# Attention and two feed-forward stages on one core: scores a slot earlier, banks emptied before the splits, three operands read in parts

## The chip, the core and the metric

The kernel runs on one core of one Trainium2 chip. TensorE (PE in the rows; PEld is its weight load) multiplies matrices into PSUM banks, VectorE (DVE), ScalarE (ACT) and GpSimd (POOL) work on tiles in SBUF, and SyncE (SP, SPq for its queue) issues the transfers. The metric is the device time of one execution in microseconds, lower is better; of several runs the median is given.

## The reference, cut to what matters

```
# attention: 4 batches x 8 heads, 768 rows of 64; chunks of 32 rows see 16 rows to the left, 8 to the right, 8 memory rows
for c in range(S // 32):
    k_full = concat([mem_k, k[:, :, max(0, 32*c - 16) : min(S, 32*c + 40)]])     # v_full alike
    a = softmax(scale * q[:, :, 32*c : 32*c + 32] @ k_full.T)
    out[:, :, 32*c : 32*c + 32] = a @ v_full
x = out, heads side by side                      # 3072 x 512
h = x @ w_in                                     # 512 -> 2048, weights in float64
x1 = softplus(h) @ w_out                         # max(h, 0) + log1p(exp(-|h|)); 2048 -> 512
a, b = x1 @ w_a, x1 @ w_b                        # 512 -> 1536 each
result = (a * b) @ w_out2                        # 1536 -> 512, float32
```

## The kernel before, in words

Every fp32 product is made of three products of rounded halves: a value is kept as a high part and a low part, and high x high, high x low and low x high are added in PSUM. So each operand has to be split: ACT writes the high part (a copy that rounds), DVE or POOL the low part (a subtraction). Weights arrive as float64 and are converted on chip: a rounding step on ACT (`top`), two bit operations on DVE (`value`), then the split (`high` on ACT, `low` on DVE).

The 3072 tokens go through in stages, with their times in the profiled execution:

- Head, 0 to 56 us: the six 64-token blocks of the first 384 tokens (class `Block`, order in the table `ROUND`), as a pipeline of scores, softmax, transposes (`flip`, tile `pat`), values (`pxb`) and `place`. `Block.place` (L380) writes the high part of x (L384) and a plain copy `xrb` (L386) on ACT and the low part on DVE (L387); `Block.store` sends `xrb` to the scratch array `x_scratch` in DRAM (L390). `FILL` adds idle-filling matmuls.
- First pass, tiles 0 to 7 of 384 tokens, 56 to 504.6 us (the last end of it 482 to 504.6): for the hidden blocks f = 0 to 9, `emit_h` (tile `ph`), `emit_soft` (softplus: three ACT steps into `e`, L591 to L593, then DVE's `g`, L595, then the split into `gh` and `gl`, L572 and L575) and `emit_x1` (tiles `px`, L608, two blocks behind). Beside that the attention of the tile that comes next runs as three 128-token units (class `Unit`) whose steps have slots, two per f, in `STEPS`, `SECOND` and `EARLY_STEPS`: `turn`, `scores` (two banks, `sc`), `soft` (eight reads of these banks by DVE, L399, and eight exponentials by ACT, L403), `norm`, `flip` (into `af`), `values` (tile `pxa`, L500), `place` (L502) and `store`. The banks of `sc`, `pa` and `pxa` share one tag, `att`, with two buffers. At the end of a tile four DVE copies (L616) take `px` out into two buffers of `e` and two of `g`, and four DMAs send them to `x_part_scratch`.
- Middle, pairs 0 to 2 of 512 + 512 tokens, 504.6 to 782.2 us: the hidden blocks 10 to 15, two at a time, by seven products in place of eight (`h_step`, three per pair; tiles `hX`, `hY`, `hW`, `hV`, L799), softplus on four results that go through two halves of one tile `et` (L894 to L899) and are split by `soft_split` (L901), and their products with `w_out` (`x1_products`, tiles `pz`, L970), to which the stored part is added (`part`, L973). The seven operands of the next pair are made from loaded x (`load_pair`, `add_pair`, `split_hi`, `split_lo`, L681).
- Pair phase, pairs 3 to 5, 782.2 to 1332.3 us: twelve `pair_step` per pair for the second feed-forward stage; on the first of them (782.2 to 964 us) the twelve weight blocks are also combined and split.

Conversion of w_a, w_b and w_out2 into `v_scratch` (class `Early`, L693: a fetch, `top` L707 on ACT, `value` L711 and L712 on DVE, a store) is spread over the first pass and the middle; `weigh` there converts w_out's blocks 10 to 15.

What sets the order: SP, PE and DVE run in the order in which the code writes their work (a `manual_schedule`), ACT and POOL too in tile 0 and from tile 7 on; between them the compiler places ACT and POOL. In the middle `order()` hangs steps on points `at(0)` to `at(12)` of an `h_step` by `put((p, s, k), ...)`. All DMAs named here go out from SP in one row, and each waits for the one eight before it (the semaphores `DMAHW0` to `DMAHW7`).

## Time and profile before

| what | value |
|---|---|
| runs shown | 1337.58, 1342.11, 1336.69 us; median 1337.58 |
| profiled execution | 1334.09 us, its span 1332.30 us |
| PE busy | 1189.3 us, 89% |
| DVE busy | 828.4 us, 62% |
| ACT busy | 559.5 us, 42% |
| POOL busy | 384.8 us, 29% |
| DMA | 226.40 MB, mean 170 GB/s |

How to read it: PE is busy through most of the span, so what can be gained lies in the stretches where it stands or runs at a lower granted clock. The view by windows gives for each stretch the busy time of each engine, the granted TensorE clock as a share of full speed and the DMA share; the view of waits gives the idle time ahead of an instruction and what released it; the timeline gives single instructions.

### The profile page before, as it was taken

Reading aid. Unit: us, or ns where it says so; the run is one execution under the profiler, and the core shown is the slowest. Engines: PE = TensorE matmul, PEld = TensorE weight load, DVE = VectorE, ACT = ScalarE, POOL = GpSimd, SP = SyncE. Lnnn points to the kernel's source line nnn. Section 1 sums busy time; section 2 is a strip of 40 time slices with the busy share of each in tenths; the row PEclk is TensorE's granted clock in tenths of the full one; section 3 lists DMA queues with packets and bytes.
Section 4 is the critical chain, followed back from the end, with each engine's and each line's share of the span. In section 5 each row is a group of like instructions: output and inputs, shape, how many; then the busy total and the mean of one; then the engine's idle time right before and its main releaser. Section 6 shows DMA issues by size and latency. Waiting matters only on the chain.

```text
span 1332.3 us, 19883 instructions
## 1 busy us (share of the span) xinstructions
PE 1189.3 (89%) x7120; PEld 1020.3 (77%) x7120; DVE 828.4 (62%) x1641; ACT 559.5 (42%) x1314; POOL 384.8 (29%) x300
## 2 busy tenths in 40 slices
PE   8588889899899987759769589999999999999999
PEld 5488879788898986547557468888888888888887
DVE  5574666566676486675575675668754666646555
ACT  5585656565675555453536524222311112221110
POOL 1000234332333473261344666547100111000000
PEclk9798999999999999779979889999999999999999
DMA  9574555464533442555756758575386643475411
GB/s 250 142 175 78 124 129 118 109 142 105 134 86 110 158 170 107 189 217 170 260 171 231 247 203 308 190 285 195 137 274 232 211 136 127 152 283 175 148 56 64
DMA packets 222643, 226.40 MB, mean 170 GB/s; under 512 B 125984, under 2 KB 165328, under 8 KB 222544
## 3 DMA queue, kind: packets, MB, share of 16 engines
q1 hardware_dynamic: 222160, 225.08, 53.3%
q8 instruction: 56, 0.92, 0.3%
q14 instruction: 43, 0.35, 0.1%
q0 software_dynamic: 384, 0.05, 0.0%
HBM read 155.09 MB, written 69.99 MB: 169 GB/s over the span
## 4 chain that ended last, share of the span: by engine, by line
PE 58%; issue 13%; ACT 8%; DMA 7%; DVE 6%; POOL 5%; SPq 3%; POOLq 0%; DVEq 0%; ACTq 0%
PE py L822 15%; PE pW L799 7%; PE pX L799 7%; PE pV L799 7%; PE ph L584 7%; PE px L608 6%; PE pY L799 4%; ACT sm L403 3%; POOL g L904 2%; PE pz L970 2%; DMA x<-x_scratch 1%; DVE af L471 1%; PE pxa L500 1%; DMA raw_b<-in_moe_w_b_dram 1%; DMA raw_a<-in_moe_w_in_dram 1%
## 5 line engine op out<-in xcount | busy, mean ns | idle before, releaser
L822 PE MATMUL py<-w2o,c 128*128 128x512 f32 (+1 forms) x870 | 218.0, 388 | 0.0
L584 PE MATMUL ph<-x,w 128*128 128x384 f32 x960 | 188.3, 345 | 11.4 <-ACT x L514 10.3
L822 PEld LDWEIGHTS py<-w2o,c 128*128 128x128 f32 x870 | 162.6, 188 | 33.5
L584 PEld LDWEIGHTS ph<-x,w 128*128 128x128 f32 x960 | 171.0, 193 | 16.2 <-ACT x L514 11.5
L608 PE MATMUL px<-gh,w 128*128 128x384 f32 x640 | 180.2, 342 | 3.0 <-DVE xo L616 1.5
L970 PE MATMUL pz<-g,w 128*128 128x512 f32 x432 | 117.2, 432 | 50.7 <-DVE part L973 29.7
L875 ACT CAST c<-r 128x512 fp32r<-128x512 f32 x36 | 22.4, 621 | 303.4 <-DVE r L873 303.4
L970 PEld LDWEIGHTS pz<-g,w 128*128 128x128 f32 x432 | 90.5, 212 | 75.9 <-DVE part L973 30.9
L608 PEld LDWEIGHTS px<-gh,w 128*128 128x128 f32 x640 | 117.9, 189 | 7.3 <-issue 3.8
L595 DVE SCALAR_TENSOR_TENSOR g<-ph,e 128x384 f32<-128x384 f32 x80 | 44.5, 556 | 116.9 <-ACT e L593 116.1
L608 PE MATMUL px<-gl,w 128*128 128x384 f32 x320 | 108.1, 338 | 5.3 <-DVE gl L575 5.1
L831 DVE TENSOR_TENSOR y<-py,y 128x512 f32<-128x512 f32 (+1 forms) x121 | 82.9, 685 | 35.8 <-PE py L822 35.6
L575 POOL TENSOR_TENSOR gl<-g,gh 128x384 fp32r<-128x384 f32 x60 | 60.9, 1015 | 148.1 <-ACT gh L572 122.8
L904 POOL TENSOR_TENSOR g<-et,g 128x512 fp32r<-128x512 f32 x36 | 48.1, 1346 | 143.8 <-ACT g L903 143.8
L471 DVE STREAM_TRANSPOSE af<-sm 32x256 f32<-32x256 f32 x180 | 78.1, 434 | 2.6
L572 ACT CAST gh<-g 128x384 fp32r<-128x384 f32 x80 | 41.1, 513 | 66.9 <-DVE g L595 66.3
L591 ACT ACTIVATE e<-ph 128x384 f32<-128x384 f32 x80 | 38.9, 486 | 70.8 <-PE ph L584 42.0
L872 DVE TENSOR_TENSOR d<-pW,q 128x512 f32<-128x512 f32 x36 | 24.9, 691 | 68.6 <-PE pW L799 68.6
L608 PEld LDWEIGHTS px<-gl,w 128*128 128x128 f32 x320 | 60.7, 190 | 6.6 <-DVE gl L575 6.1
L403 ACT ACTIVATE sm<-sm,st 128x96 f32<-128x96 f32 x168 | 60.4, 363 | 3.4 <-DVE st L399 3.4
L758 POOL TENSOR_TENSOR u<-t,u 128x512 fp32r<-128x512 f32 x30 | 43.2, 1445 | 43.6 <-ACT u L754 43.6
L799 PE MATMUL pW<-xs,u 128*128 128x512 f32 x216 | 54.8, 389 | 0.0
(203 smaller groups left out, 2347.1 us busy)
## 6 DMA issues: line engine op xcount, KB each, us to landing
...
```

Of the source, the lines that this page charges most:

```text
L403: nc.scalar.activation(sm[:, h], sm[:, h], AF.Exp, bias=st[:, 0, h:h + 1], scale=-1.0, accum_out=st[:, 1, h:h + 1])
L471: nc.vector.transpose(out=af[32 * kb:32 * kb + 32, x], in_=self.sm[32 * x:32 * x + 32, :, 32 * kb:32 * kb + 32])
L575: engine.tensor_tensor(lo, val, hi.bitcast(F32), ALU.subtract)
L584: nc.tensor.matmul(ph, lhsT=w[:, a, kt * P:(kt + 1) * P], rhs=x[:, c, kt, :], start=n == 0, stop=n == 3 * KT - 1)
L595: nc.vector.scalar_tensor_tensor(g, ph, 0.0, e, ALU.max, ALU.add)
L608: nc.tensor.matmul(acc[t][i][:, :TT], lhsT=a, rhs=c, start=f == 0 and m == 0, stop=f == FA - 1 and m == 2)
L758: engine.tensor_tensor(u[:, :, 1], self.source(i), u[:, :, 0].bitcast(F32), ALU.subtract)
L799: nc.tensor.matmul(bank[:, :T2], lhsT=u[:, j, a, kt * P:kt * P + P], rhs=x[kt][:, c], start=first_ and m == 0, stop=m == 3 * KH - 1, skip_ ...
L822: nc.tensor.matmul(b, lhsT=c[:, x, r], rhs=w[:, y, cols], start=n == 0, stop=n == 3 * GROUP - 1)
L831: tt(y, b, y, ALU.add)
L904: nc.gpsimd.tensor_tensor(g[:, 1], e, g[:, 0].bitcast(F32), ALU.subtract)
L970: nc.tensor.matmul(b[:, :T2], lhsT=a, rhs=c, start=f == FA and m == 0, stop=f == NF1 - 1 and m == 2)
```

## The change

The change has six parts.

1. Tables. The scores of the units come a slot or more earlier, the third unit is placed at slot 17 of a tile (18 before), and the steps of the first six units have new slots. The conversion halves that ran inside the first units' softmax (`weigh` of class `Unit`) are gone from there; `convert()` runs them all.
2. `Unit.place` writes the low part from PSUM on DVE for every tile; before, it did so for t < 2 only, and POOL did it from the plain copy for the others.
3. `Block.place` makes no plain copy on ACT. POOL adds the two parts into spare buffers, and `store_first` sends them to `x_scratch` in three DMAs at slot 1 of tile 0. One half of `packed[1]` loads into the buffers of `loaded[0]`.
4. `store_parts` sends the two parts of x of each tile to a new scratch array (two DMAs of 786 KB per tile), and `load_parts` reads the operands "11", "12" and "22" of pairs 0 to 2 from it as parts. For these no `split_hi` and `split_lo` remain; of the other four, ACT writes all the high parts and DVE all the low ones.
5. `h_step` has two `et` tiles (four halves); the softplus steps that read PSUM stand ahead of the splits, and the low parts go to POOL and DVE in turn.
6. In the middle, `load_pair` and `add_pair` of the next pair come earlier, one `Early` conversion is made per `h_step` in place of two to four, and the remaining 15 move to the first eight steps of the pair phase. `weigh` runs three times in tile 7 (two before) and three times in pair 0 (four before).

```
-PLACED = (5, 12, 18)
+PLACED = (5, 12, 17)
-STEPS = {0: ((-13, "turn"), (-9, "scores"), (-8.9, "soft"), (-7, "norm"), (-5, "flip"), ...
+STEPS = {0: ((-13, "turn"), (-10, "scores"), (-9.9, "soft"), (-8, "norm"), (-6, "flip"), ...
...
     class Block:
             nc.scalar.copy(xh, self.px)
-            self.raw = raw = wp.tile([P, KT, QB], F32, tag="w", name=f"xrb{u}")
-            nc.scalar.copy(raw, self.px)
             nc.vector.tensor_tensor(xl, self.px, xh.bitcast(F32), ALU.subtract)
-        def store(self):
-            nc.sync.dma_start(xd[:, :, QB * self.u:QB * self.u + QB], self.raw)
+            n, k, i = [x[u] for x in ((3, 3, 3, 2, 2, 1), (0, 0, 0, 1, 1, 2), (0, 1, 2, 0, 1, 0))]
+            if i == 0:
+                pool, tag = ((a2, "kt"), (a2, "qt"), (wp, "w"))[k]
+                first[k] = pool.tile([P, KT, n * QB], F32, tag=tag, name=f"xrb{u}", **({"bufs": 1} if k < 2 else {}))
+            nc.gpsimd.tensor_tensor(first[k][:, :, i * QB:i * QB + QB], xh.bitcast(F32), xl.bitcast(F32), ALU.add)
...
     class Unit:
-            if t < 2:
-                nc.scalar.copy(xh, self.px)
-                nc.vector.tensor_tensor(xl, self.px, xh.bitcast(F32), ALU.subtract)
-                nc.scalar.copy(raw, self.px)
-            else:
-                nc.scalar.copy(raw, self.px)
-                nc.scalar.copy(xh, self.px)
-                nc.gpsimd.tensor_tensor(xl, raw, xh.bitcast(F32), ALU.subtract)
+            nc.scalar.copy(xh, self.px)
+            nc.vector.tensor_tensor(xl, self.px, xh.bitcast(F32), ALU.subtract)
+            nc.scalar.copy(raw, self.px)
...
+    def store_first():
+        for k, c0, n in ((0, 0, 3 * QB), (1, 3 * QB, 2 * QB), (2, 5 * QB, QB)):
+            nc.sync.dma_start(xd[:, :, c0:c0 + n], first[k])
+    def store_parts(t):
+        for c in range(2):
+            nc.sync.dma_start(xhl[:, :, c, TT * t:TT * t + TT], xt[t][:, c].bitcast(F32))
+    plan.append((1, -1, store_first))
+    plan += [(2 * FA * t + 1.1, -1, partial(store_parts, t)) for t in range(NTILE - 1)]
...
+    def load_parts(p, n):
+        sums[p, n] = operand(p, n)
+        t, k = {"11": (0, 0), "12": (0, 1), "22": (1, 1)}[n]
+        c0 = (2 * p + t) * T2
+        (x,) = sums[p, n]
+        for i in range(KH):
+            nc.sync.dma_start(x[:, i].bitcast(F32), xhl[:, KH * k + i, :, c0:c0 + T2])
...
     def h_step(p, s, at, between):
-        et = wp.tile([P, 2, T2], F32, tag="w", name=f"et{p}_{s}")
+        es = [wp.tile([P, 2, T2], F32, tag="w", name=f"et{p}_{s}_{n}") for n in range(2)]
         product(x, p, f, "12", False)
         soft_e(x, e1)
         soft_g(r, e0)
-        soft_split(p, 1, f1, e0)
         at(4)
         product(w, p, f, "22", False)
         tt(d21, w, q, ALU.add)
+        soft_hi(p, 1, f1, e0)
+        soft_lo(p, 1, f1, e0, nc.gpsimd)
+        soft_e(d21, e2)
+        soft_g(x, e1)
         at(5)
         product(v, p, f, "s4", False)
         tt(q, v, q, ALU.add)
-        soft_g(x, e1)
-        soft_e(d21, e0)
-        soft_split(p, 0, f0, e1)
-        soft_g(d21, e0)
-        soft_e(q, e1)
-        soft_split(p, 1, f0, e0)
-        soft_g(q, e1)
-        soft_split(p, 0, f1, e1)
+        soft_hi(p, 0, f0, e1)
+        soft_e(q, e3)
+        soft_lo(p, 0, f0, e1, nc.vector)
+        soft_g(d21, e2)
+        soft_hi(p, 1, f0, e2)
+        soft_lo(p, 1, f0, e2, nc.gpsimd)
+        soft_g(q, e3)
+        soft_hi(p, 0, f1, e3)
+        soft_lo(p, 0, f1, e3, nc.vector)
...
         for p in range(NPAIR):
-                for k in (0, 2) + (() if s + 1 < NS else (5, 7)):
-                    if pre:
-                        e = pre.pop(0)
-                        put((p, s, k), e.fetch)
-                        put((p, s, k + 4), e.top, e.value)
-                        put((p, s, k + 5), e.store)
-            put((p, NS - 1, 1), partial(load_pair, p + 1))
-            for k, n in ((7, "11"), (8, "s2"), (8, "s3"), (9, "s1"), (10, "12"), (11, "22"), (12, "s4")):
+                e = pre.pop(0)
+                put((p, c, 1), e.fetch)
+                put((p, c, 6), e.top, e.value)
+                put((p, c, 8), e.store)
+            put((p, 1, 5), partial(load_pair, p + 1))
+            if p + 1 < NPAIR:
+                for k, n in ((1, "11"), (5, "12"), (6, "22")):
+                    put((p, 2, k), partial(load_parts, p + 1, n))
+                names = ((7, "s2"), (8, "s3"), (11, "s1"), (12, "s4"))
...
+        for n, e in enumerate(pre):
+            for k, step in ((0, e.fetch), (3, e.top), (4, e.value), (5, e.store)):
+                k += 7 * (n // 2) + 2 * (n % 2)
+                put(("g", k // 7, k % 7), step)
```

Three places in the order, before and after. The rows give the line, the operation with its tiles and shapes, and the semaphores waited for.

First the end of the head. On SP before (`raw` is a weight in float64, `kn` keys of a later tile, the `xrb` rows left out are the other four of six):

```order
L116 DMA raw_196<-in_moe_w_out_dram 128x1024 [waits DMAHW4_49]
L390 DMA x_scratch<-xrb_432 512x1x64 [waits DMAHW5_49,Activation_49]
...
L390 DMA x_scratch<-xrb_638 512x1x64 [waits DMAHW2_49,Activation_49]
L116 DMA raw_655<-in_moe_w_in_dram 128x4x256 [waits DMAHW3_49,DVE_49]
L116 DMA raw_738<-in_moe_w_out_dram 128x1024 [waits DMAHW4_49,PE_49]
L201 DMA kn_78<-in_k_dram 32x12x32 [waits DMAHW5_49]
```

On SP now:

```order
L117 DMA raw_194<-in_moe_w_out_dram 128x1024 [waits DMAHW4_49]
L117 DMA raw_644<-in_moe_w_in_dram 128x4x256 [waits DMAHW5_49,PE_49,Activation_49]
L549 DMA x_scratch<-xrb_431 512x1x192 [waits DMAHW6_49,Pool_49]
L549 DMA x_scratch<-xrb_587 512x1x128 [waits DMAHW7_49,Pool_49]
L549 DMA x_scratch<-xrb_629 512x1x64 [waits DMAHW0_49,Pool_49]
L117 DMA raw_730<-in_moe_w_out_dram 128x1024 [waits DMAHW1_49,DVE_49,PE_49]
L553 DMA x_parts_scratch<-x_428 512x1x384 [waits DMAHW2_49,Activation_49]
L553 DMA x_parts_scratch<-x_428 512x1x384 [waits DMAHW3_49,DVE_49]
```

And DVE there, before (`work` holds a block's scores and sums, `scb` is the bank of its scores; the last block):

```order
L407 TENSOR_SCALAR work_375<-work_375 128x4 [waits Activation_49]
L408 RECIPROCAL work_375<-work_375 128x4 [waits DVE_49]
L410 TENSOR_TENSOR work_375<-work_375 128x384 [waits DVE_49]
L387 TENSOR_TENSOR x_430<-pxb_479,x_430 128x4x64 [waits PE_49,Activation_49]
L399 ISA work_438<-scb_439,mask_72 128x96 [waits DMAHW5_49]
```

DVE at the same place now:

```order
L412 TENSOR_SCALAR work_373<-work_373 128x4 [waits Activation_49]
L413 RECIPROCAL work_373<-work_373 128x4 [waits DVE_49]
L415 TENSOR_TENSOR work_373<-work_373 128x384 [waits DVE_49]
L390 TENSOR_TENSOR x_428<-pxb_477,x_428 128x4x64 [waits Activation_49]
L404 ISA work_436<-scb_437,mask_72 128x96
```

A block's `work` took the buffer of an `xrb` that a DMA was still reading, and DVE waited for that DMA; now no wait for a DMA stands there.

Second the end of a tile of the first pass, on DVE before (`xo` and `g` from `px` are the tile's results on their way out, `ph_2` the third hidden block of the next tile, `sc_10` a bank of scores):

```order
L595 SCALAR_TENSOR_TENSOR g<-ph_1_2221,e_1_2234 128x384 [waits Activation_49,Pool_49]
L471 STREAM_TRANSPOSE af<-sm_2093 32x256 [waits PE_49]
L471 STREAM_TRANSPOSE af<-sm_2093 32x256 x4
L616 COPY xo_0_2258<-px_0_1648 128x384 [waits DMAHW3_49,DVE_49,PE_49]
L616 COPY xo_1_2261<-px_1_1649 128x384 [waits DMAHW4_49,DVE_49,PE_49]
L616 COPY g<-px_2_1650 128x384 [waits PE_49,Pool_49]
L616 COPY g<-px_3_1651 128x384 [waits PE_49,Pool_49]
L595 SCALAR_TENSOR_TENSOR g<-ph_2_2286,e_2_2299 128x384 [waits DMAHW4_49,DVE_49,Activation_49]
L399 ISA sm_2306,st_2307<-sc_10_2268,mask_72 128x96 [waits DMAHW5_49,PE_49]
```

DVE at the same place now:

```order
L476 STREAM_TRANSPOSE af<-sm_2077 32x256 x5
L601 SCALAR_TENSOR_TENSOR g<-ph_1_2222,e_1_2235 128x384 [waits Activation_49,Pool_49]
L622 COPY xo_0_2274<-px_0_1667 128x384 [waits DMAHW4_49,DVE_49,PE_49]
L622 COPY xo_1_2277<-px_1_1668 128x384 [waits DMAHW5_49,DVE_49,PE_49]
L622 COPY g<-px_2_1669 128x384 [waits PE_49,Pool_49]
L622 COPY g<-px_3_1670 128x384 [waits PE_49,Pool_49]
L404 ISA sm_2284,st_2285<-sc_10_2244,mask_72 128x96
```

The reads of `sc_10` stood behind the `g` of `ph_2`; now they stand ahead of it.

Third the end of pair 0, on DVE before (`val` is a converted weight, `x`, `xs`, `xa` are operands of pair 1, `part` the sums over the hidden blocks):

```order
L899 SCALAR_TENSOR_TENSOR et_2_5994<-hq_2_6002,et_2_5994 128x512 [waits DVE_49,Activation_49]
L711 TENSOR_SCALAR val_o_6106<-raw_o_6031 128x512 [waits DMAHW3_49]
L712 SCALAR_TENSOR_TENSOR val_o_6106<-raw_o_6031,val_o_6106 128x512 [waits DVE_49,Activation_49]
L681 TENSOR_TENSOR x_1_6129<-x_1_6014,x_1_6129 128x2x512 [waits DMAHW7_49,Activation_49]
L711 TENSOR_SCALAR val_a_6165<-raw_a_6076 128x512 [waits DMAHW7_49,DMAHW6_49]
L712 SCALAR_TENSOR_TENSOR val_a_6165<-raw_a_6076,val_a_6165 128x512 [waits DVE_49,Activation_49]
L681 TENSOR_TENSOR xs_1_6148<-x_1_6018,xs_1_6148 128x2x512 [waits Pool_49]
L973 TENSOR_TENSOR part_0_0_6044<-pz_0_0_5962,part_0_0_6044 128x512 [waits DMAHW4_49,PE_49]
```

DVE at the same place now:

```order
L913 SCALAR_TENSOR_TENSOR et_2_1_5999<-hq_2_6007,et_2_1_5999 128x512 [waits DVE_49,Activation_49]
L921 TENSOR_TENSOR g_0_15_6099<-et_2_1_5999,g_0_15_6099 128x512 [waits Activation_49]
L725 TENSOR_SCALAR val_o_6103<-raw_o_6019 128x512 [waits DMAHW1_49]
L726 SCALAR_TENSOR_TENSOR val_o_6103<-raw_o_6019,val_o_6103 128x512 [waits DVE_49,Activation_49]
L695 TENSOR_TENSOR xs_1_6123<-xs_6021,xs_1_6123 128x2x512 [waits Activation_49]
L695 TENSOR_TENSOR xs_1_6141<-x_1_5937,xs_1_6141 128x2x512 [waits Activation_49]
L994 TENSOR_TENSOR part_0_0_6049<-pz_0_0_5969,part_0_0_6049 128x512 [waits DMAHW4_49,DMAHW3_49,PE_49]
```

Between the last softplus and the first `part` stood two conversions and two low parts of operands; now stand there a low part of the softplus, one conversion and two low parts of operands.

## Rows read from the trace of the kernel before

**Rows 1.** Windows, one a stage: length, busy (x instructions) by engine, PEclk, DMA share, GB/s.

```profile
0.00:56.00 56.00, 34.16 (x449) 25.54 (x449) 25.95 (x129) 25.76 (x83) 5.95 (x19) 0.82 0.76 202
56.00:125.00 69.00, 59.20 (x624) 55.86 (x624) 47.09 (x130) 51.69 (x134) 2.16 (x4) 0.93 0.59 135
125.00:482.00 357.00, 326.23 (x2739) 308.47 (x2737) 218.69 (x696) 219.24 (x650) 127.70 (x111) 0.99 0.48 122
482.00:504.60 22.60, 17.46 (x97) 16.50 (x97) 22.50 (x22) 9.06 (x20) 15.87 (x11) 1.00 0.66 241
504.60:605.10 100.50, 69.72 (x261) 54.60 (x260) 66.93 (x76) 51.06 (x85) 39.52 (x22) 0.81 0.45 158
605.10:693.70 88.60, 67.62 (x271) 53.08 (x270) 54.77 (x58) 41.70 (x68) 32.22 (x18) 0.90 0.58 205
693.70:782.20 88.50, 67.96 (x272) 53.34 (x271) 54.63 (x58) 45.63 (x76) 48.06 (x31) 0.88 0.62 220
782.20:964.00 181.80, 181.80 (x804) 150.54 (x803) 124.60 (x164) 58.17 (x106) 97.44 (x78) 1.00 0.62 229
```

**Rows 2.** Waits of the head, all engines: total us, times, longest us.

```profile
PE pat L370 <- ACT x L384: 20.2, 2, 19.7
...
DVE work L399 <- DMA x_scratch<-xrb: 18.0, 1, 18.0
```

**Rows 3.** Timeline of the head: start, us, instruction, idle time before and releaser.

```profile
36.38 12.80 SPq L390 DMA_DIRECT2D x_scratch<-xrb  x3
44.90 0.26 DVE L399 CUSTOM_DVE_ANT_0 work<-scb,mask 128x96 f32<-128x96 f32 x1 [17.98 <-DMA x_scratch<-xrb]
...
48.47 1.06 PE L370 MATMUL pat<-ident,work 128*96 128x128 f32 x4 [19.66 <-ACT x L384]
```

**Rows 4.** Waits of PE in tiles 0 to 7.

```profile
PE pxa L500 <- issue: 21.9, 8, 4.8
PE ph L584 <- ACT x L514: 10.3, 4, 3.5
```

**Rows 5.** Timeline at the start of tile 3.

```profile
197.24 0.49 ACT L591 ACTIVATE e<-ph 128x384 f32<-128x384 f32 x1 [4.35 <-DMA x_part_scratch<-xo]
...
198.87 0.56 DVE L595 SCALAR_TENSOR_TENSOR g<-ph,e 128x384 f32<-128x384 f32 x1 [2.28 <-ACT e L593]
199.34 0.25 DVE L399 CUSTOM_DVE_ANT_0 sm<-sc,mask 128x96 f32<-128x96 f32 x1
...
200.23 0.98 PE L500 MATMUL pxa<-af,vn 96*64 96x64 f32 x26 [2.57 <-issue]
```

**Rows 6.** Waits of PE in the middle.

```profile
PE pz L970 <- DVE part L973: 29.7, 3, 10.3
PE hX L799 <- ACT hq L915: 14.4, 4, 10.2
PE pz L970 <- POOL g L904: 12.9, 3, 5.6
```

**Rows 7.** Timeline of DVE at the end of pair 0.

```profile
579.31 1.52 DVE L711 TENSOR_SCALAR val_o<-raw_o 128x512 uint32<-128x512 uint32 x1
...
582.45 3.41 DVE L681 TENSOR_TENSOR x<-x,x 128x1024 fp32r<-128x1024 f32 x1
585.78 2.58 DVE L711 TENSOR_SCALAR val_a<-raw_a 128x512 uint32<-128x512 uint32 x1
588.47 2.67 DVE L712 SCALAR_TENSOR_TENSOR val_a<-raw_a,val_a 128x512 uint32<-128x512 uint32 x1
...
594.33 2.47 DVE L973 TENSOR_TENSOR part<-pz,part 128x512 f32<-128x512 f32 x4
...
601.80 0.42 DVE L711 TENSOR_SCALAR val_b<-raw_b 128x512 uint32<-128x512 uint32 x1
602.32 0.69 DVE L712 SCALAR_TENSOR_TENSOR val_b<-raw_b,val_b 128x512 uint32<-128x512 uint32 x1
...
605.88 1.22 DVE L681 TENSOR_TENSOR xb<-x,xb 128x1024 fp32r<-128x1024 f32 x1
```

More of the change, by code (lines that the diff above doesn't have):

```diff
@@ L29 @@
              (0, "place"), (1, "store")),
-         2: ((-13, "turn"), (-9, "scores"), (-8.9, "soft"), (-7, "norm"), (-5, "flip"), (-3, "flip2"), (-0.1, "values"),
-             (0, "place"), (0.9, "store"))}
-SECOND = (((15, "turn"), (20, "scores"), (20.1, "soft"), (22, "norm"), (23, "flip"), (25, "flip2"), (26.9, "values"),
+         2: ((-12, "turn"), (-8, "scores"), (-7.9, "soft"), (-6, "norm"), (-4, "flip"), (-3, "flip2"), (-0.1, "values"),
+             (0, "place"), (1, "store"))}
+SECOND = (((15, "turn"), (19, "scores"), (19.1, "soft"), (21, "norm"), (22, "flip"), (24, "flip2"), (26.9, "values"),
@@ L41 @@
+EARLY_STEPS = (((4, "scores"), (4.1, "soft"), (5, "normal"), (8, "flip_p"), (10.9, "values"), (11, "place"), (12, "store")),
+               ((6, "scores"), (6.1, "soft"), (7, "normal"), (12, "flip_p"), (13.9, "values"), (14, "place"), (15, "store")),
+               ((9, "scores"), (9.1, "soft"), (10, "normal"), (15, "flip_p"), (16.9, "values"), (17, "place"), (18, "store")))
 EARLY = len(EARLY_STEPS)
-FETCHED = (2, 3, 4, 5)
+FETCHED = (3, 4, 5, 6)
 ROUND = ((2, "normal"), (4, "place"), (None, "top"), (0, "scores"), (1, "soft"), (None, "low"), (None, "value"),
-         (2, "flip"), (3, "values"), (None, "high"), (4, "store"))
+         (2, "flip"), (3, "values"), (None, "high"))
@@ L276, in load @@
             t = self.t
-            kp = wp.tile([P, 4, 4, D], F32, tag="w", name=f"kp{t}_{half}")
-            qp = wp.tile([P, 4, 4, D], F32, tag="w", name=f"qp{t}_{half}")
+            if t == 1 and half == 0:
+                kp, qp = [x.rearrange("p k n s -> p (k n s)")[:, :1024].rearrange("p (h r d) -> p h r d", h=4, r=4)
+                          for x in (loaded[0].k, loaded[0].q)]
+            else:
+                kp = wp.tile([P, 4, 4, D], F32, tag="w", name=f"kp{t}_{half}")
+                qp = wp.tile([P, 4, 4, D], F32, tag="w", name=f"qp{t}_{half}")
             self.raw[half] = kp, qp
@@ L909, in h_step @@
         f0, f1 = FA + 2 * s, FA + 2 * s + 1
-        et = wp.tile([P, 2, T2], F32, tag="w", name=f"et{p}_{s}")
-        e0, e1 = et[:, 0], et[:, 1]
+        es = [wp.tile([P, 2, T2], F32, tag="w", name=f"et{p}_{s}_{n}") for n in range(2)]
+        e0, e1, e2, e3 = [es[n // 2][:, n % 2] for n in range(4)]
         x = bank("acc3" if (p, s) == (0, 1) else "h", f"hX{p}_{s}")
@@ L1065, in order @@
         LAST = NTILE - 1
-        for s, at in ((0, 3), (1, 6)):
-            put(("t", at - 3), cvs[NF2 + s].fetch)
-            for k, step in enumerate(cvs[NF2 + s].slots()):
+        for c, at in ((0, 3), (1, 6)):
+            put(("t", at - 3), cvs[NF2 + c].fetch)
+            for k, step in enumerate(cvs[NF2 + c].slots()):
                 put(("t", at + k), step)
-        for n, at in ((0, 2), (1, 4)):
+        for n, at in ((0, 2), (1, 4), (2, 8)):
             put(("t", at), partial(weigh, FA + n, ("t", at + 4), ("t", at + 5), ("t", at + 7), ("t", at + 8)))
-        put(("t", 1), partial(load_pair, 0))
+        put(("t", 1), partial(store_parts, LAST), partial(load_parts, 0, "11"), partial(load_pair, 0))
@@ L1078, in order @@
+        put(("t", 10), partial(load_parts, 0, "12"))
         put(("t", 17), cvs[NF2 + 2].fetch)
[L1080 to L1082 removed]
+        put((0, 0, 0), partial(load_parts, 0, "22"))
+        put((0, 0, 2), partial(split_hi, 0, "s4", nc.scalar.copy), partial(split_lo, 0, "s4", nc.vector))
         for k, step in enumerate(cvs[NF2 + 2].slots()):
@@ L1107, in order @@
+            for k, n in names:
+                put((p, 2, k), partial(split_hi, p + 1, n, nc.scalar.copy))
+                low = partial(split_lo, p + 1, n, nc.vector)
+                if n != "s4":
+                    put((p, 2, k), low)
                 elif p + 1 < NPAIR:
                     put((p + 1, 0, 0), low)
-            put((p, NS - 1, 3), partial(load_part, p, 0))
-            put((p, NS - 1, 9), partial(load_part, p, 1))
-        assert not pre
+            put((p, 2, 3), partial(load_part, p, 0))
@@ L1112, in order @@
+            put((p, 2, 9), partial(load_part, p, 1))
         P2 = NPAIR - 1
@@ L1179, in at @@
                     if p == NPAIR:
+                        run("g", f, k)
                         for g, kk in ((f + 1, 7 + k), (f + 2, k)):
@@ L1216, in order @@
                         x1_products(NPAIR - 1, 1, i, range(FA, NF1))
+        assert not todo, sorted(todo)
         while jobs:
```

58 lines of the change are left out of this document (25 added, 33 removed).

## The prediction, made before the changed kernel ran

> **What bounds the kernel now.** I read the windows first, one for each stage [rows 1]. PE is busy in 1189.3 of 1332.3 us, so the question is where the other 143 are, and where PE runs at a lower granted clock. The first pass of the pair phase (782.2 to 964) has neither: 181.80 of 181.80 us busy at clock 1.00, 804 matmuls, that is 0.226 us each. This is my measure for a full matmul. The head leaves PE idle for 56.0 − 34.2 = 21.8 us, tile 0 for 9.8, tiles 1 to 7 for 30.8, the end of the first pass for 5.1, pairs 0, 1 and 2 for 30.8, 21.0 and 20.5. In the pairs the granted clock is 0.81 to 0.90 besides: 261 matmuls at 0.226 are 59.0 us where pair 0 takes 100.5, so 41.5 are lost; pairs 1 and 2 lose 27.4 and 27.0 in the same way. Of these 95.9 us, 72.3 are idle and 23.6 are matmuls at a lower clock (an estimate, as some matmuls are narrower and some records may be missing).
>
> Then I read the waits and the timeline at the places where PE stands. In the head one wait carries nearly all: PE stands 19.7 us because a block's softmax is late, and that because DVE waited 18.0 us for a store of `xrb` [rows 2]. The timeline shows why [rows 3]: three of the six stores are issued from 36.38 on, behind the weight fetches in SP's row, and DVE reads the scores of the last block only at 44.90. In the first pass PE waits 21.9 us ahead of `pxa`, eight times, and 10.3 us for the x of the next tile [rows 4]. One such place is shown [rows 5]: ACT's `e` waits 4.35 us for the store of `xo`, DVE's `g` behind it starts at 198.87, the reads of the score bank behind that at 199.34, and PE, which needs the bank, at 200.23, 2.57 us late. In the middle three waits make 57.0 of the 72.3 idle us: `part` on DVE 29.7, `hq` on ACT 14.4, the low parts on POOL 12.9 [rows 6].
>
> **The change part by part.** The sum is made against the profiled execution, 1334.1 us (its span of 1332.3 and 1.8 around it); the median of the runs stands 3.5 above it.
>
> Head: −18. No buffer that DVE needs is read by a store any more, so the 18.0 us of DVE's wait [rows 2] go. POOL gets six additions and works 5.95 of 56 us there [rows 1], ACT loses six copies. The three stores wait for POOL, in SP's row behind weight fetches; behind them stand more weights and the parts of x, which nothing needs within the next tile. What is late next is the fetch of the first weights; it isn't bounded by a row better than by the wait itself, so the term lies between 0 and −19.7.
>
> Tile 0: −8. Idle 9.8 us plus 7% of 69 us at clock 0.93, some 4.8 [rows 1]. The conversions leave the first units' softmax, yet they all still have to be made by ACT, which is busy 51.7 of 69 us. I take about half; bounds 0 and −13.
>
> Tiles 1 to 7: −19. The reads of the score bank now stand ahead of the `g` that waits for the store, so the 2.57 us of rows 5 shrink to the end of the four copies ahead of them. Of the 21.9 us, 4.8 are in tile 0 [rows 4], so 17.1 are left; I take 13. The third unit is placed a slot earlier, so the 10.3 us for x shrink as well; I take 6. DVE gets the low part of 18 units more: at 0.56 us for 384 columns [rows 5] some 0.75 each, 13 us in a stage in which it has 138 to spare [rows 1]. Writing the parts of x is 12.6 MB more over 426 us, 30 GB/s; at the 122 GB/s for a share of 0.48 [rows 1] it adds 0.12 to the DMA share, which stays below 0.6. These stores stand in SP's row ahead of those of `xo`, but come a slot earlier. Bounds −28 and +5 (if the `xo` stores land later and hold `e` longer).
>
> End of the first pass: −4 of 5.1 idle us. DVE is busy 22.50 of 22.60 there [rows 1] and loses seven of the ten operand copies and low parts, each about 1.22 us [rows 7]. Bounds 0 and −5.1.
>
> Middle: −50. At the end of pair 0 DVE works from 579.31 to 594.33 before it comes to `part`, with instructions that POOL's work makes long: a low part takes 3.41 us there and 1.22 alone, a conversion 2.58 + 2.67 and 0.42 + 0.69 alone [rows 7]. In the new order one conversion, two low parts and a softplus low part stand there, 1.11 + 2 × 1.22 + 0.69 = 4.2 us when POOL is quiet, and POOL's own additions have moved away. That would free more than the 10.3 us of the longest wait; as POOL still works at times I take 20 of the 29.7. `hq`: ACT makes four high parts per pair in place of seven, two of them still just ahead of `hq`: 7 of 14.4. POOL makes half the low parts of the softplus: 9 of 12.9. Together 36 of the 72.3 idle us. If the matmuls at a lower clock shrink in the same proportion, 12 of 23.6, and 2 of the smaller waits come with it, that is −50: some −16, −18 and −16 for the pairs. The added wait here is SP's: the load of operand "11" waits for PE's last use of its only buffer, and the loads of "12" and "22" and of the next weights queue behind it; PE makes that last use in the first product of the same step, so it holds SP for a few us. The loads add 9.4 MB over 277.6 us, 34 GB/s, to shares of 0.45 to 0.62. Bounds: −90, and +5 if these loads are late at each pair.
>
> Pair phase: +8. Fifteen conversions come to its first eight steps. DVE has 181.8 − 124.6 = 57.2 us to spare [rows 1], 38 of them in eight of twelve steps. A conversion costs DVE 1.11 us alone and 5.25 beside POOL [rows 7], so 17 to 79 us in all. POOL is busy 54% of the time there [rows 1]: 0.46 × 1.11 + 0.54 × 5.25 = 3.3 us, 50 in all, 12 over the spare time; the four later steps take up some of that. Bounds 0 and +41 (79 less 38). On this the Trainium skill has a rule, "SBUF — State Buffer", section "SBUF: two separate sides": a DVE instruction in a two-port mode, or one with two SBUF inputs, and a GpSimd instruction lock each other out of a shared port for the whole instruction. The rows of 2.58 against 0.42 us agree with it; by the rule alone, with every conversion colliding, the term would be the +41 of the bound.
>
> Sum: −18 − 8 − 19 − 4 − 50 + 8 = −91, so 1243 us against the profiled execution and 1246.6 as a median; I say 1246.
>
> **The rivals.**
> The middle stays chained (0.20): the conversions, high parts and softplus steps have the same engines, and the wait moves from `part` to the last softplus. For it speaks that ACT's chain ahead of `hq` is only shortened; against it the 15.0 us in rows 7. The middle gives −20, the sum is −61: 1277.
> Nearly all gaps close (0.12): full clock comes back with them. Head −19, tile 0 −13, tiles −27, end −5, middle −80, pair phase 0: −144, so 1194. Against it speaks that each term would be at its bound.
> The head keeps its gap (0.10), because the fetches of weights and not the stores decide when the last blocks run: −73, so 1265. For it speaks a DMA share of 0.76 in the head [rows 1].
> DVE becomes the bound in the pair phase (0.08): +41 in place of +8, −58, so 1280.
> Slower than before (0.04): DVE's chain goes over the pair phase's time, PE stands in every step, and the granted clock, 1.00 there, falls towards its lower level of 1.2 GHz, half of 2.4. The other terms give −99; twelve steps of 181.8 us lose that when they take 281, at a mean clock of 0.65. The lowest of any stage is 0.81, with PE idle for 31% of it [rows 1]. At 0.60 the price is +121: 1334 − 99 + 121 + 3.5, so about 1360.
> The forecast has 0.46.
>
> **How the numbers follow.** The forecast's own range is 1222 to 1268. The range of 8 in 10 reaches up to the two rivals of 1277 and 1280 and down to near that of 1194: 1200 to 1288. Out of it fall the case of 1360, more than half of that of 1194 and the tails, together under 2 in 10. A difference of 0.5% is 6.7 us and is about what a measurement can tell here. All cases but the last are faster by more than that; for a sum of several of them at once I leave 0.02 for no change and 0.04 for slower, 0.94 for faster.
>
> **What would show it.** Head: no wait for a store ahead of the last block's score reads, PE's gap under 3 us, the window to the end of the head some 38 us long. Tiles: `pxa` waits below 1 us where they were 2.57. Middle: pairs of about 84, 71 and 72 us, the `part` wait below 4 us at each end, clock nearer 0.9 in pair 0. Pair phase: PE busy near 100% and 190 us long, DVE near 95% in its first two thirds. The prediction is wrong if the middle is longer than 250 us, or if the pair phase's first twelve steps take more than 200 us.

## The result, and the profile after

The changed kernel takes 1253.84 us (median of four runs, 1251.35 to 1256.14), the kernel before 1337.13 us in the same comparison: a ratio of 0.9372, with a 95% interval of 0.9339 to 0.9404. The profiled execution's span went from 1332.3 to 1251.1 us, 81.2 less. The ratios leave out a run far above the others of its kernel: there is one, of g3 below, at 4058.29 us.

The windows of the profile after, by stages that begin and end at the same work as those of [rows 1] (columns as there; the twelve steps of the pair phase's first pair end at 877.7, those of before at 959.0):

```profile
0.00:37.00 37.00, 32.49 (x448) 24.21 (x448) 26.07 (x130) 24.24 (x78) 7.41 (x20) 1.00 0.96 250
37.00:108.60 71.60, 60.42 (x629) 55.73 (x629) 47.99 (x130) 51.81 (x134) 5.51 (x10) 0.95 0.76 188
108.60:461.60 353.00, 326.96 (x2734) 312.31 (x2733) 227.87 (x713) 218.69 (x650) 107.22 (x93) 0.97 0.58 160
461.60:481.40 19.80, 17.56 (x99) 16.60 (x98) 18.69 (x18) 13.26 (x25) 15.59 (x11) 1.00 0.50 177
481.40:560.00 78.60, 62.74 (x259) 51.01 (x259) 49.01 (x67) 42.29 (x73) 23.73 (x15) 0.89 0.63 226
560.00:623.60 63.60, 62.09 (x271) 50.44 (x270) 37.85 (x53) 35.70 (x60) 18.29 (x10) 1.00 0.76 273
623.60:691.00 67.40, 62.71 (x272) 50.40 (x271) 44.51 (x55) 42.52 (x71) 34.77 (x23) 1.00 0.64 230
691.00:877.70 186.70, 181.47 (x782) 148.28 (x781) 144.93 (x187) 64.11 (x117) 100.50 (x79) 0.98 0.78 284
```

Stage by stage, forecast beside what was found (lengths from the first matmul of a stage to that of the next, so not quite those of the windows of before):

| stage | before | after | change | forecast |
|---|---|---|---|---|
| head | 55.9 | 37.0 | −18.9 | −18 |
| tile 0 | 69.3 | 71.5 | +2.2 | −8 |
| tiles 1 to 7 | 356.8 | 353.1 | −3.7 | −19 |
| end of the first pass | 22.6 | 19.8 | −2.8 | −4 |
| middle | 277.5 | 209.6 | −67.9 | −50 |
| pair phase | 550.1 | 560.1 | +10.0 | +8 |

In the head the wait for a store is gone; what is left of the 20.2 us of [rows 2] is the first row below. The other rows are PE's waits in tiles 1 to 7 (109 to 462 us), then in the middle (482 to 691 us):

```profile
PE pat L375 <- ACT x L389: 2.9, 3, 1.4
...
PE sc L458 <- DVE qt L442: 8.3, 3, 3.6
PE pxa L501 <- issue: 5.7, 6, 1.0
PE ph L590 <- ACT x L509: 5.6, 3, 4.1
PE ph L590 <- DVE g L601: 4.5, 1, 4.5
...
PE hX L813 <- ACT hq L932: 10.4, 1, 10.4
PE hW L813 <- DVE hr L943: 4.8, 2, 3.7
PE pz L991 <- DVE part L994: 3.6, 2, 2.4
```

Ahead of `pxa` PE waits at most 1.0 us in these tiles (2.57 in rows 5). But it waits 8.3 us for the queries' transposes, `qt`, a wait that the kernel before does not have. DVE's waits for weights in the same stretch point to the cause (18.3 us in these two rows, 4.9 in the same two before), and the timeline shows one place of three (columns as in rows 3):

```profile
DVE val_b L725 <- DMA raw_b<-in_moe_w_b_dram: 10.1, 2, 5.4
DVE val_a L725 <- DMA raw_a<-in_moe_w_in_dram: 8.2, 2, 5.1
```

```profile
257.20 0.68 ACT L721 ACTIVATE raw_b<-raw_b 128x512 f32<-128x512 f32 x1 [4.11 <-DMA raw_b<-in_moe_w_b_dram]
257.20 0.43 DVE L725 TENSOR_SCALAR val_b<-raw_b 128x512 uint32<-128x512 uint32 x1 [5.41 <-DMA raw_b<-in_moe_w_b_dram]
...
260.51 0.56 DVE L601 SCALAR_TENSOR_TENSOR g<-ph,e 128x384 f32<-128x384 f32 x1 [1.48 <-ACT e L599]
...
262.54 0.67 DVE L442 STREAM_TRANSPOSE qt<-qn 128x512 f32<-128x512 f32 x1
...
263.36 0.89 PE L458 MATMUL sc<-kt,qt 64*64 64x96 f32 x32 [3.60 <-DVE qt L442]
```

DVE comes to a conversion 5.4 us before its weights have landed and, as its order is fixed, does nothing else. ACT stands at the same weights for 4.1 us, its softplus behind them is late, and DVE waits another 1.48 us for that. So the transposes are late, and PE waits 3.6 us for them.

It is DVE that comes sooner; the fetches take no longer. One fetch of the kernel before and the same one now, each with its conversion:

```profile
325.97 0.39 SPq L700 DMA_DIRECT2D raw_b<-in_moe_w_b_dram  x1
331.24 0.43 DVE L711 TENSOR_SCALAR val_b<-raw_b 128x512 uint32<-128x512 uint32 x1 [1.95 <-DMA raw_b<-in_moe_w_b_dram]
...
306.56 0.39 SPq L714 DMA_DIRECT2D raw_b<-in_moe_w_b_dram  x1
311.48 0.43 DVE L725 TENSOR_SCALAR val_b<-raw_b 128x512 uint32<-128x512 uint32 x1 [4.72 <-DMA raw_b<-in_moe_w_b_dram]
```

From the issue to the conversion pass 5.3 us before and 4.9 now (5.3 to 6.1 and 4.4 to 6.4 over all conversions of this stage at which DVE stands). But DVE stands there from 3.3 us after the issue before, and from 0.2 us now.

The wait of 4.5 us for `g` in the list has another cause. Near the end of the stage ACT's `e` waits 10.0 us for a store of `xo`, which stands in SP's row behind the parts of x; the last row is the same place in f1, a kernel without parts that comes below:

```profile
439.80 0.81 SPq L623 DMA_DIRECT2D x_part_scratch<-xo  x2
448.71 0.49 ACT L597 ACTIVATE e<-ph 128x384 f32<-128x384 f32 x1 [10.00 <-DMA x_part_scratch<-xo]
450.95 2.29 PE L590 MATMUL ph<-x,w 128*128 128x384 f32 x6 [4.55 <-DVE g L601]
...
440.28 0.49 ACT L596 ACTIVATE e<-ph 128x384 f32<-128x384 f32 x1 [4.32 <-DMA x_part_scratch<-xo]
```

In the pair phase DVE stands at conversions again (timeline at the third step):

```profile
718.46 0.43 DVE L725 TENSOR_SCALAR val_o<-raw_o 128x512 uint32<-128x512 uint32 x1 [2.66 <-DMA raw_o<-in_moe_w_out_dram]
...
723.53 0.73 PE L836 MATMUL py<-w2o,c 128*128 128x512 f32 x2 [1.81 <-ACT c L889]
```

DVE stands 2.66 us at a conversion, the product `c` behind it comes late, and PE waits 1.81 us for its next sum. A second such place is at 817 us. The two make all 5.2 us that PE is idle in the twelve steps, and matmuls at a lower clock (a mean of 0.98) the other 4.7 of the 10 us.

### The profile page after: what moved, and what is told of

It reads as the page before. It is cut to its first block, busy times and chain, and to the rows that moved or that the text cites. A ratio compares the mean times of both kernels' runs of the same rounds, so it can differ in the third digit from the quotient of the medians.

```text
span 1251.1 us, 19880 instructions
## 1 busy us (share of the span) xinstructions
PE 1176.6 (94%) x7120; PEld 1015.5 (81%) x7120; DVE 815.1 (65%) x1668; ACT 552.5 (44%) x1305; POOL 328.9 (26%) x264
## 4 chain that ended last, share of the span: by engine, by line
PE 56%; DMA 6%; DVE 6%; ACT 4%; issue 3%; SPq 2%; POOL 1%; DVEq 0%; POOLq 0%; ACTq 0%
PE py L836 14%; PE pW L813 7%; PE pV L813 7%; PE pX L813 6%; PE pz L991 5%; PE px L614 4%; PE ph L590 4%; PE pY L813 3%; DMA v<-v_scratch 2%; DMA raw_o<-in_moe_w_out_dram 1%; PE hW L813 1%; PE hV L813 1%; PE hX L813 1%; DMA xb<-x_parts_scratch 1%; ACT et L909 1%
## 5 line engine op out<-in xcount | busy, mean ns | idle before, releaser
L836 PE MATMUL py<-w2o,c 128*128 128x512 f32 (+1 forms) x870 | 221.1, 391 | 5.2 <-ACT c L889 2.9
L590 PE MATMUL ph<-x,w 128*128 128x384 f32 x960 | 192.1, 350 | 10.2 <-ACT x L509 5.6
L991 PE MATMUL pz<-g,w 128*128 128x512 f32 x432 | 101.6, 392 | 5.2 <-DVE part L994 3.6
L991 PEld LDWEIGHTS pz<-g,w 128*128 128x128 f32 x432 | 80.9, 188 | 24.7 <-DVE part L994 4.4
L813 PE MATMUL pX<-x,u 128*128 128x512 f32 x216 | 54.8, 389 | 0.0
L813 PE MATMUL pX<-xa,u 128*128 128x512 f32 x216 | 54.8, 389 | 0.0
```

What stands on the lines that cost most here:

```text
L590: nc.tensor.matmul(ph, lhsT=w[:, a, kt * P:(kt + 1) * P], rhs=x[:, c, kt, :], start=n == 0, stop=n == 3 * KT - 1)
L813: nc.tensor.matmul(bank[:, :T2], lhsT=u[:, j, a, kt * P:kt * P + P], rhs=x[kt][:, c], start=first_ and m == 0, stop=m == 3 * KH - 1, skip_ ...
L836: nc.tensor.matmul(b, lhsT=c[:, x, r], rhs=w[:, y, cols], start=n == 0, stop=n == 3 * GROUP - 1)
L991: nc.tensor.matmul(b[:, :T2], lhsT=a, rhs=c, start=f == FA and m == 0, stop=f == NF1 - 1 and m == 2)
```

## The experiments

Theory W, formed on these rows: what the change lost or failed to gain (tiles 1 to 7, the pair phase) comes from conversions at which DVE arrives before the weights. Rivals: the first unit's scores come too early for their transposes (S), DVE was given too much in the first pass (C) or in the pair phase (D). For the middle: its gain comes from h_step's new order (H), from the conversions that left it (E), or from reading parts. Each kernel was timed beside the kernel before, whose median was 1333.06 to 1334.64 us in these comparisons, so kernels are best compared by their ratios. As a measure of noise: four kernels with the same first pass (the changed one, e1, f2, f3) took 353.1, 348.8, 348.9 and 349.1 us for tiles 1 to 7, and 71.5 to 74.7 for tile 0. So the change is worth 4 to 8 us in tiles 1 to 7, if the one profile of the kernel before is as typical. Lengths of stages are from one profile of each kernel.

**e1: pair phase, value later after its fetch.**

```
-            for k, step in ((0, e.fetch), (3, e.top), (4, e.value), (5, e.store)):
+            for k, step in ((0, e.fetch), (6, e.top), (7, e.value), (8, e.store)):
```

> The changed kernel, with one edit: in the pair phase each of the 15 moved conversions is rounded, computed and stored three points later after its fetch (6, 7, 8 for 3, 4, 5), so that its weights have three more points (some 6 us) to land. The same work, the same number of instructions. Theory W (the pair phase lost 10 us because DVE, in its fixed order, stands at a conversion whose weights have not landed, and the products behind it come late, at 723 and 817 us, each time followed by matmuls at a lower clock): both jams go, the twelve steps take 177 to 179 us in place of 187, the kernel about 1244 to 1246. Rival D (DVE has too much work there, with POOL making its instructions long): the work is the same, so the twelve steps stay at 184 to 187 us and the kernel within 3 us of 1254.

Measured 1244.93 us, ratio 0.9341 (0.9314 to 0.9369). The interval overlaps that of the changed kernel; the stage is clearer. The twelve steps take 181.7 us, half of the loss gone. DVE's waits for weights are no longer in the list of waits; it waits for the buffers of earlier values instead, whose stores have not ended, 13.7 us in all (6.5 in the changed kernel):

```profile
688.00:869.70 181.70, 179.01 (x781) 147.42 (x780) 139.49 (x187) 64.10 (x117) 101.09 (x78) 0.99 0.83 292
...
DVE val_b L725 <- DMA v_scratch<-val_a: 6.8, 3, 4.9
...
DVE val_a L725 <- DMA v_scratch<-val_o: 4.3, 2, 4.1
```

**e2: first pass, value later after its fetch.**

```
-PRE_STEPS = (0, 3.4, 4.1, 4.3)
+PRE_STEPS = (0, 5.2, 5.9, 6.1)
```

> The changed kernel, with one edit: in the first pass the 18 conversions are rounded, computed and stored 1.8 slots later after their fetch (5.2, 5.9, 6.1 for 3.4, 4.1, 4.3). Theory W (tiles 1 to 7 gained only 4 us, because DVE waits 18 us for weights in its fixed order, and the transposes of a unit's queries come late behind that): DVE's waits for raw weights fall from 18 to below 4 us, PE's wait for qt from 8.3 to below 2, tiles 1 to 7 take 344 to 348 us in place of 353. Rival S (the scores of a tile's first unit were moved to a slot at which its transposes, three slots behind turn, cannot be ready): the wait for qt stays at 7 to 9 us, the stage at 352 to 354.

Measured 1240.40 us, ratio 0.9306 (0.9279 to 0.9334). Tiles 1 to 7 take 336.9 us, a gain larger than W had asked for. DVE's waits for the fetches are gone from the list, PE's wait for `qt` is down to 3.1 us:

```profile
109.80:446.70 336.90, 322.79 (x2736) 309.15 (x2733) 227.51 (x713) 217.44 (x648) 105.15 (x93) 0.98 0.61 167
```

```profile
PE pxa L501 <- issue: 6.6, 6, 1.5
PE sc L458 <- DVE qt L442: 3.1, 6, 0.9
```

Rival S falls: the scores stand where they stood, and DVE has the same work (227.5 us). PE's idle time falls by 11.9 us: 5.2 by `qt`, 5.6 by the wait for x, and 2.3 by the wait for `g` behind the store of `xo`, of which W had said nothing. The edit moves the stores of the values too, so it shows that the conversions' points cost this time, and not which of their steps.

**e3: the first unit's scores at their old slots.**

```
-STEPS = {0: ((-13, "turn"), (-10, "scores"), (-9.9, "soft"), (-8, "norm"), (-6, "flip"), (-4, "flip2"), ...
+STEPS = {0: ((-13, "turn"), (-9, "scores"), (-8.9, "soft"), (-7, "norm"), (-5, "flip"), (-3, "flip2"), ...
```

> The changed kernel, with one edit: the steps scores, soft, norm, flip and flip2 of a tile's first unit go back to the slots that they had before (-9, -8.9, -7, -5, -3). Rival S: the wait for qt goes, 8.3 us less, and as the softmax then still has time, tiles 1 to 7 take about 345. Theory W: the wait for qt goes here too, as the transposes get one slot more, but DVE's waits for weights stay at about 18 us, and what was waited for is waited for elsewhere: the reads of the score bank or pxa come later again, the stage takes 350 to 354.

Measured 1254.53 us, ratio 0.9429 (0.9385 to 0.9474). The stage takes 348.4 us, inside the noise. The wait for `qt` is gone, the one ahead of `pxa` is 10.5 us (5.7), and DVE still waits 25.5 us for weights in four rows: the wait only changed its place, as W has it, and S, which had asked for 345, falls.

**e4: place as before.** The edit puts back the old branch of `Unit.place` (plain copy first, low part on POOL for t of 2 and more).

> The changed kernel, with one edit: Unit.place as before (for tiles 2 to 7 a plain copy first, and the low part from it on POOL). Theory W: DVE has 18 x 0.68 = 12 us less to do, but stands at the same conversions; PE's wait for qt stays within 2 us of 8.3, and the x of the next tile comes later, as POOL's part is about 1.3 us: tiles 1 to 7 take 353 to 357 us. Rival C (DVE was given too much in the first pass): the wait for qt shrinks below 4 us, the stage to 347 to 350.

Measured 1253.73 us, ratio 0.9409 (0.9381 to 0.9437). DVE is busy 215.5 us in tiles 1 to 7, 12 less, and the stage takes 352.0; the wait for `qt` is 9.4 us. Rival C falls, and part 2 of the change shows no worth of its own here.

**f1: no parts.** `store_parts` and `load_parts` go; 11, 12 and 22 are split as the other operands. One place of the edit:

```
-            if p + 1 < NPAIR:
-                for k, n in ((1, "11"), (5, "12"), (6, "22")):
-                    put((p, 2, k), partial(load_parts, p + 1, n))
-                names = ((7, "s2"), (8, "s3"), (11, "s1"), (12, "s4"))
-            else:
-                names = ((7, "11"), (8, "s2"), (8, "s3"), (10, "s1"), (11, "12"), (12, "22"), (12, "s4"))
+            names = ((7, "11"), (8, "s2"), (8, "s3"), (10, "s1"), (11, "12"), (12, "22"), (12, "s4"))
```

> The changed kernel without part 4: no store_parts, and the operands 11, 12 and 22 of pairs 0 to 2 are split on chip again (high parts on ACT, low parts on DVE, at the points that the changed kernel uses for pair 3). All else stays. Theory W (in the first pass the weights of the conversions land late, among other reasons because 12.6 MB of parts go out in the same row of transfers): tiles 1 to 7 take 342 to 348 us in place of 349 to 353; rival: the fetch stands behind the next tile's keys and queries in SP's row anyway, 349 to 353. For the middle: if reading parts is what freed the ends of the pairs, it takes 225 to 240 us in place of 210; if the order of h_step or the fewer conversions did, 208 to 216.

Measured 1251.99 us, ratio 0.9387 (0.9362 to 0.9412): not to be told from the changed kernel. The middle takes 214.7 us (5 more), the end of the first pass 22.3 (2.5 more), tile 0 and tiles 1 to 7 take 70.0 and 345.7 (1.5 and 3 to 7 less). DVE still waits 21 us for weights there, so the parts do not cost the first pass by way of these. One place is the store of `xo` shown above: the longest wait for it is 4.3 us here (10.0), and PE's wait of 4.5 us for `g` is gone. That PE wait stands in every kernel with parts (2.2 to 4.7 us) and in neither without (f1, g3). The rest was not settled. Tiles 1 to 7 and the middle of f1:

```profile
107.40:453.10 345.70, 323.37 (x2735) 309.10 (x2734) 228.02 (x712) 218.97 (x649) 107.30 (x93) 0.99 0.49 125
475.40:690.10 214.70, 190.91 (x799) 153.86 (x799) 138.12 (x181) 127.28 (x211) 75.93 (x47) 0.94 0.55 197
```

**f2: h_step as before.** The edit puts back the old `h_step` and `soft_split`.

> The changed kernel without part 5: h_step as before (one et tile of two halves, splits between the softplus steps, all their low parts on POOL). Theory H (of the 68 us that the middle gained, 18 more than forecast, a large share comes from emptying the banks first and sharing the low parts, since two halves of et chained the four softplus): the middle takes 235 to 250 us in place of 210. Rival E (the conversions that left the middle did it): 210 to 220.

Measured 1275.12 us, ratio 0.9573 (0.9551 to 0.9595). The middle takes 230.9 us, 21 more, a little under H's range and over E's:

```profile
481.40:712.30 230.90, 196.48 (x800) 156.00 (x799) 121.48 (x157) 121.77 (x204) 100.68 (x66) 0.92 0.61 219
```

**f3: the conversions in the middle again.** The edit puts back the old loop over `(0, 2)` and `(5, 7)` with its fetch, top, value and store.

> The changed kernel with the 24 conversions made in the middle again, at the points of before, and none in the pair phase. Theory W for the pair phase: its twelve steps take 177 us in place of 187 (176.8 before). For the middle: theory E gives 235 to 255 us in place of 210, as the conversions stand in DVE's order ahead of part and hq again; theory H 215 to 225.

Measured 1260.14 us, ratio 0.9453 (0.9432 to 0.9475). The middle takes 227.1 us, 17.5 more, between the two ranges, and the pair phase has lost nothing:

```profile
477.30:704.40 227.10, 193.31 (x800) 155.10 (x799) 148.34 (x204) 129.63 (x219) 75.11 (x48) 0.94 0.77 273
704.40:881.20 176.80, 176.80 (x782) 146.40 (x781) 119.53 (x159) 55.60 (x102) 97.91 (x78) 1.00 0.64 235
```

So neither H nor E alone: undone one at a time they cost 21, 17.5 and 5 us of the 67.9. The other 24 may belong to the earlier loads and sums, or to parts that only work together; that was not taken apart.

**f4: the head alone.** The kernel before with part 3 of the change.

> The kernel before with part 3 alone: no plain copy in Block.place, POOL's additions into spare buffers, three stores at slot 1 of tile 0, one half of packed[1] in the buffers of loaded[0]. The head ends at 37 us in place of 56 whatever the theory. Theory K (tile 0 got no faster, 71.6 us in place of 69.3, since with the head 19 us shorter the weight fetches have less time and ACT has to make the same conversions in the rest): tile 0 takes 71 to 75 us with the old tables too, the kernel 15 to 18 us less than before. Rival T (the new tables of the first units cost it): tile 0 takes 68 to 70 us, the kernel 18 to 20 us less.

Measured 1314.82 us, ratio 0.9874 (0.9857 to 0.9892), 18.2 us less.

```profile
0.00:37.00 37.00, 32.63 (x448) 24.44 (x448) 26.06 (x129) 24.26 (x78) 7.41 (x20) 1.00 0.96 248
37.00:108.80 71.80, 60.08 (x625) 56.22 (x625) 47.97 (x131) 52.05 (x133) 5.52 (x10) 0.93 0.65 160
108.80:459.70 350.90, 328.66 (x2738) 312.01 (x2738) 218.42 (x696) 218.69 (x649) 127.91 (x111) 0.97 0.49 124
```

Tile 0 takes 71.8 us with the old tables, in K's range and 1.8 over T's; the kernels with one and the same tile 0 differ by 3 us, so this favours K and does not settle it. Of K's reason the trace shows little: ACT stands 4.0 us at weights in tile 0 here, but 0.3 in the changed kernel. Tiles 1 to 7 take 350.9 us with the old tables, so the new tables gained nothing to be seen there while the weights were late. PE's two waits there, with the old tables:

```profile
PE pxa L504 <- issue: 16.3, 6, 3.6
PE ph L593 <- ACT x L518: 3.2, 3, 1.6
```

The wait ahead of `pxa` stays, so the tables removed it (it is 6.0 with the new tables and the old place, e4); the one for x shrinks without them (10.3 before).

**g1, g2: both late points, then pair 0 relieved.** g1 joins the edits of e1 and e2. g2 also moves the conversions that stand at the end of pair 0's first h_step into the second:

```
-        for n, (c, k) in enumerate(((0, 1), (0, 3), (1, 0))):
-            put((0, c, k), partial(weigh, FA + 3 + n, (0, c, k + 3), (0, c, k + 3), (0, c, k + 5), (0, c, k + 5)))
+        for n, (c, k, d) in enumerate(((0, 1, 1), (0, 3, 3), (1, 0, 5))):
+            put((0, c, k), partial(weigh, FA + 3 + n, (0, 1, d), (0, 1, d), (0, 1, d + 2), (0, 1, d + 2)))
...
-                put((p, c, 6), e.top, e.value)
-                put((p, c, 8), e.store)
+                put((p, c, 6) if p + c else (0, 1, 2), e.top, e.value)
+                put((p, c, 8) if p + c else (0, 1, 4), e.store)
```

> The changed kernel with both later points for the conversions (first pass 5.2, 5.9, 6.1; pair phase 6, 7, 8). Theory W: the two gains are in different stages and add: 13 us from the first pass's edit and 5 us from the pair phase's, some 1234 to 1238, a ratio to the kernel before of 0.925 to 0.929. Rival: a shorter first pass moves transfers into the middle, and less than half of the smaller gain is left: 1238 to 1241.

> As g1_both_late, and in pair 0 the conversions that stand between the first and the second h_step (w_out's blocks 13 to 15 and one of the second stage's weights) move into the second h_step. Theory Q (the 10.4 us that PE waits for hq in pair 0, in this kernel as in the one before, are ACT standing at a high part of w_out whose value DVE has not made yet): the wait falls below 3 us, pair 0 takes 68 to 71 us in place of 79, the kernel 1225 to 1229. Rival: the softplus of the first step itself is late, as POOL and DVE make its low parts until 506: the wait stays above 7 us, and the kernel stays at 1234 to 1238.

g1: 1232.61 us, ratio 0.9239 (0.9205 to 0.9272); the gains add, within the noise (0.0031 and 0.0066 of the ratio alone, 0.0133 together). g2: 1238.21 us, ratio 0.9273 (0.9230 to 0.9315), no better. The wait for `hq` fell from 10.4 to 4.3 us, but one for `hr` took its place, and the middle takes 211.9 us against g1's 211.1: Q named the wait rightly in the main (it had said below 3 us) and its worth wrongly. PE's waits of g2 from 470 to 555 us:

```profile
PE hW L813 <- DVE hr L943: 8.0, 2, 6.2
PE hX L813 <- ACT hq L932: 4.3, 1, 4.3
```

**g3: g2 without parts.** The edits of f1 on g2.

> As g2_pair0_relief, and without the parts of x (operands 11, 12 and 22 split on chip, no store_parts). With the conversions' weights landing in time, the 12.6 MB of parts cost the first pass less than the 3 to 7 us seen in f1_no_parts, while the middle still pays some 5 us and the end of the first pass 2 us for the splits: if so, 2 to 7 us slower than g2_pair0_relief. Rival: the transfers' load still costs the first pass as much: within 2 us of it or faster.

1234.73 us, ratio 0.9231 (0.9188 to 0.9275). Tile 0 and tiles 1 to 7 take 70.7 and 331.0 us (75.9 and 336.9 in g2), the middle 214.4: the expected loss of 2 to 7 us did not come, and the parts give and take the same within the noise, once more.

**g4: g2 with a third buffer for converted values** (`bufs=3` for the tag `tmp`).

> As g2_pair0_relief, with three buffers in place of two for the converted values (tag tmp). In e1_pair_late_value DVE waits 13.7 us in the pair phase for the stores of earlier values out of these buffers. If these waits make what is left of the jams (181.7 us for twelve steps, 176.8 before), the twelve steps take 177 to 179 us and the kernel 3 to 5 us less than g2_pair0_relief; if the collisions with POOL do, nothing changes.

1229.82 us, ratio 0.9222 (0.9188 to 0.9256), the lowest median of the versions tried, 7.8% under the kernel before; its interval overlaps those of g1, g2 and g3. The stage that the edit aims at is clearer: the twelve steps take 182.1 us in g2, and here what they took before the change, PE without a gap, with all fifteen conversions in them:

```profile
682.10:864.20 182.10, 179.01 (x781) 147.38 (x780) 141.86 (x187) 64.08 (x117) 100.84 (x78) 0.99 0.82 292
...
676.20:853.00 176.80, 176.80 (x782) 146.40 (x781) 139.89 (x187) 64.05 (x117) 104.52 (x78) 1.00 0.83 300
```

## Why the prediction was right, and where not

**Total.** Right: 1246 against 1253.84, inside 1200 to 1288 and inside the forecast's own 1222 to 1268. The terms were less good than their sum: the changes of tile 0 and tiles 1 to 7 came out 25.5 us short, and the middle 17.9 us over. That the sum fits is in part luck.

**Head, −18.** Right in cause and size; f4 shows it by itself. The limit that I couldn't bound (the first weights) did not show: the DMA share is 0.96, and PE's gaps there are at most 1.4 us. (The score reads that waited 18.0 us before were those of the fifth of the six blocks; the last block's followed at 49.0.)

**Tile 0, −8: wrong, +2.2.** The step that failed is "I take about half" of the idle and slow time. The idle time did not fall (11.2 us, 9.8 before): the wait ahead of `pxa` shrank from 6.5 to 2.7 us, but PE now waits for other steps of ACT:

```profile
PE sc L324 <- ACT af L491: 3.1, 1, 3.1
PE pa L490 <- ACT xr L511: 2.9, 2, 1.7
PE pxa L501 <- issue: 2.7, 1, 2.7
```

One reason that offers itself is that the head's gap of 19 us had served to fetch weights. It is not shown: the DMA share of tile 0 is 0.76 in place of 0.59, but 0.65 with the head alone (f4), and ACT waits 0.3 us for weights in tile 0 of the changed kernel. f4 is as long there with the old tables, so what holds tile 0 at this length stays open.

**Tiles 1 to 7, −19: mis-sized, −3.7.** The two waits that I named shrank, `pxa` by 9.6 us (15.3 to 5.7 outside tile 0) where I had said 13, the x by 4.7 where I had said 6; but the x is no merit of the third unit's earlier place, as it shrinks in f4 too. What failed is that nothing was said to be late next but the store of `xo`: DVE runs in a fixed order and now comes sooner to the conversions (at the fetch shown above 0.2 us after its issue, 3.3 before). Their weights set the new limit. The store of `xo` that the bound of +5 had named did come later at one place, for 4.5 us of PE's time. With 1.8 more slots for the conversions (e2) the stage is 336.9 us, 19.9 below before, about the term of −19; as f4 has 5.9 of these with the old tables, not all of it need be the tables' own.

**End of the first pass, −4.** Measured −2.8; without the parts (f1) 2.5 of it are lost again, as the cause that I gave has it.

**Middle, −50: mis-sized, −67.9.** The waits went as I had it for `part` (29.7 to 3.6 us; I had left 9.7) and for POOL's low parts (12.9 us, gone from the list); `hq` fell only from 14.4 to 10.4. Twelve of the 18 us more are idle time: it fell by 50.2 us (72.3 to 22.1) where the terms gave 38, with 6 more for `part`, 4 for POOL's low parts, 5 for the smaller waits, and 3 less for `hq`. The other 6 are the clock: the step "if the matmuls at a lower clock shrink in the same proportion" was too careful. With 2 and 7% idle in pairs 1 and 2 the granted clock is 1.00 there, not 0.90 and 0.88, and PE takes 62.1 and 62.7 us for what was 67.6 and 68.0. Which part of the change did it is shown for 44 of the 67.9 us (f1, f2 and f3, each undone alone); the rest is open.

**Pair phase, +8.** The size is right (+10.0) by luck, the cause is wrong. (The 181.8 us of my measure reach past the twelve steps, which took 176.8.) I counted DVE's instructions made long by POOL; their means are 0.64 to 0.87 and 0.94 to 1.12 us, under 2 us a conversion in place of my 3.3. That makes 27 us in all, less than the 38 to spare, so my own sum gives 0 with it. DVE is busy 77% of the first two thirds and not 95%. What jammed was the wait for weights, and behind it the wait for buffers (e1, g4; without conversions, f3, nothing is lost). The rule of the Trainium skill ("SBUF — State Buffer", "SBUF: two separate sides") fits the single long rows of [rows 7], but every conversion colliding, the bound that I took from it, was never near, and with landed weights DVE has room for all fifteen.

**Rivals.** The middle did not stay chained, and the clock of the pair phase stayed at 0.98. "Nearly all gaps close" at 1194 came nearer to the middle than the forecast did, and was far off in the first pass.
